# x loaded from the scalar engine's queue, its statistics taken from a copy spread over the partitions, and a shorter PE program: a one-token attention and MLP block on one core

## The chip, the cores and the metric

The kernel runs on one core of one Trainium2 chip. The metric is the device time of one execution in microseconds (us); the core is the only one, so its span is what counts. Lower is better. The engines are named as in the profile: PE (matrix products), PEld (PE's weight loads), DVE (vector), ACT (scalar), POOL (GpSimd) and SP (sync, which here issues transfers). Transfers between HBM and the core's memory run on 16 DMA engines.

## The reference

One token x of 512 numbers is normalised, goes through attention with 32 query heads over a cache of 8 key/value heads of 65536 positions, and beside it through a small MLP; the three are summed.

```python
xn = _layernorm(x)                               # (x - mean) / sqrt(var + 1e-5)
q = (xn @ wq).reshape(B, Sq, Hq, Dh)             # 512 -> 32 heads x 128
scores = einsum("bhqd,bhkd->bhqk", q, k) * Dh ** -0.5
o = einsum("bhqk,bhkd->bhqd", softmax(scores), v)
attention = o.reshape(B, Sq, Hq * Dh) @ wo       # 4096 -> 512
mlp = relu(xn @ w1) @ w2                         # 512 -> 1792 -> 512
return x + attention + mlp
```

All of it is f32. k and v together are 537 million bytes; wq, wo, w1 and w2 are the rest of the 561 MB that the kernel reads.

## The kernel before

The 8 x 65536 cache positions are cut into 32 chunks of 16384 (`NCH`). Two buffers of 128 partitions x 64 KB, `kt` and `vt`, hold one chunk of k and one of v; `kt` first holds wq and last wo, and a third buffer, `wt`, first holds w1 and last w2. There are no copies of these buffers: a buffer is loaded again as soon as its last reader is done, and one is filled while the other is read.

Every engine has its own program, and the order between engines is written out by hand with semaphores. `take(e, sem, n)` makes engine e wait until a semaphore has reached n and takes n off; `after(ins, sem, n)` makes an instruction wait for n; `link` chains POOL's instructions one after another, `next_of` ACT's.

- SP issues all transfers, in this order: the first part of wq (line 151, ahead of the section in which the engines run), xT and xrow (lines 162 and 163: x as 128 partitions x 4 numbers, and x as one row), the other two parts of wq (line 160), w1 (line 164), then k and v in turns (lines 166 to 175), each behind its `kfree` or `vfree`, then wo, w2 and the store of y (line 183).
- POOL fills constants first (lines 195 to 210: `minus` and `plus`, 128 x 128 matrices of -1/512 and 1/512; `eps`; the identity), ends the layer norm (lines 211 to 218: one Newton step on the reciprocal root, xn, and xn into `qpad`), and scales the four quarters of w1 by xn and adds them (lines 223 to 228).
- ACT begins the layer norm on xT (lines 238 to 248): it sums each partition's four numbers, PE multiplies the sums by `minus` (line 267), which gives every partition the negative mean; ACT centres x, squares and sums again, PE multiplies by `plus` (line 268), and ACT adds eps and takes the root. Then ACT copies xrow into `x4`, loads the table for Exp, and in its loop computes the exponentials of each chunk.
- PE runs a loop of 34 turns, `turns`. Turn t multiplies what lies in `kt` by `qpad` (line 314: wq in turn 0, k in turns 1 to 32, wo in turn 33), 8 rounds of 4 products into two pairs of PSUM banks. In turns 2 to 33 there stands ahead of that the second half of the chunk before: the maximum over the partitions (lines 277 and 278), three passes of the MLP's product that give the same result each turn (line 282), the product with `vt` (line 293) and the sums (lines 300 and 303). A hint at the head of the loop is tied to a branch near the end of the program that is always taken.
- DVE clears PSUM (`banks`, line 373), takes the reciprocal root (line 374), transposes PE's scores out of PSUM (line 367), computes the maxima and keeps the running sums. In turn 0 the transposes wait for the third part of wq before they give the banks back (`turn_scores(["wq2", "wq2"])`).

Of the kernel before, what the change touches and what calls it, by code (L numbers as in the profile page):

```python
# [8 lines left out]
AF = mybir.ActivationFunctionType  # L9
# [3 lines left out]
P = 128  # L13
D = 512
# [21 lines left out]
NCH = SK // CHUNK  # L36
NB = CHUNK // P
XA = D // P
WIDE = 4
ROUNDS = 8  # L40
WQ_CUTS = [4096, 4096, 8192]
WQ_SEMS = ["ends", "k", "wq2"]
# [7 lines left out]
def take(e, sem, n=1):  # L50

    return e.sem_inc(sem, -n).wait_op(sem, n, "sem-ge")  # L52
# [7 lines left out]
def attention_and_mlp_kernel(  # L60
# [11 lines left out]
    nc = tc.nc  # L72
    sp, pe, dve, act, pool = nc.sync, nc.tensor, nc.vector, nc.scalar, nc.gpsimd
    scale = float(DH) ** -0.5

    def sbuf(name, *shape):
        return nc.alloc_sbuf_tensor(name, list(shape), F32).ap()
# [3 lines left out]
    def sem(name):  # L81
        if name not in sems:
            sems[name] = nc.alloc_semaphore(name)
        return sems[name]

    def after(ins, name, n=1):

        return ins.wait_op(sem(name), n, "sem-ge")

    kt = sbuf("kt", P, CHUNK)  # L90
# [7 lines left out]
    xrow = sbuf("xrow", 1, D)  # L98
    x4 = sbuf("x4", P, D)
    ident = sbuf("ident", P, P)  # L100
    ones = sbuf("ones", P, P)
    minus = sbuf("minus", P, P)
    plus = sbuf("plus", P, P)
    eps = sbuf("eps", P, 1)
    sel = sbuf("sel", P, WIDE, GROUP)
    xT = sbuf("xT", P, XA)
    st = sbuf("st", P, 8)
    xc = sbuf("xc", P, XA)
    sq = sbuf("sq", P, XA)
    xn = sbuf("xn", P, XA)  # L110
    qpad = sbuf("qpad", P, 32)
    qall = sbuf("qall", P, NQ)
# [15 lines left out]
    banks = nc.alloc_psum_tensor("banks", [P, 8 * 512], F32).ap()  # L128
    pair = [banks[:, i * 1024 : (i + 1) * 1024] for i in range(2)]
    acc = banks[:, 2048:2560]  # L130
    pma = banks[:, 2560:3072]
    lo_new = pma[:, 256 : 256 + 2 * GROUP].rearrange("p (t g) -> p t g", g=GROUP)
    pmb = banks[:, 3072:3584]
    y4 = banks[:, 3584:]
    hrow = y4[:, : FB * 32]
    yacc = acc[:, :P]

    wq_row = wq[0].rearrange("p a n -> p (a n)")
    wo_row = wo[0].rearrange("d j n -> d (j n)")
# [14 lines left out]
    tc.declare_fence(pool.nop().ins, group="first")  # L154
    section = ctx.enter_context(ExitStack())
    inside = section.enter_context(tc.tile_critical(sync_engine=mybir.EngineType.Pool, no_gpsimd_drain=True))  # L156
    for i in range(len(WQ_CUTS)):
        cut = slice(wq_at[i], wq_at[i + 1])
        if i:
            sp.dma_start(kt[:, cut], wq_row[:, cut]).then_inc(sem(WQ_SEMS[i]), 16)  # L160
        else:
            sp.dma_start(xT, x.rearrange("(p a) -> p a", p=P)).then_inc(sem("x"), 16)  # L162
            sp.dma_start(xrow, x.rearrange("(o n) -> o n", o=1)).then_inc(sem("xrow"), 16)  # L163
    sp.dma_start(wt, w1_row).then_inc(sem("w1"), 16)
    take(sp, sem("kfree"))
    sp.dma_start(kt, k[0, 0]).then_inc(sem("k"), 16)
# [8 lines left out]
    for i in range(len(WO_CUTS)):  # L175
        cut = slice(wo_at[i] * D, wo_at[i + 1] * D)
        sp.dma_start(kt[:, cut], wo_row[:, cut]).then_inc(sem(f"wo{i}" if i else "k"), 16)
    sp.wait_ge(sem("hT"), 1)
    for i in range(len(W2_CUTS)):
        cut = slice(w2_at[i] * D, w2_at[i + 1] * D)  # L180
# [7 lines left out]
    def link(ins):  # L188

        if chain[0]:  # L190
            after(ins, "pool", chain[0])
        chain[0] += 1
        return ins.then_inc(sem("pool"), 1)

    pool.memset(minus, -1.0 / D)
    pool.memset(plus, 1.0 / D)
    pool.memset(eps, EPS).then_inc(sem("means"), 1)
    link(pool.memset(ident, 0.0))
    link(pool.affine_select(
# [8 lines left out]
    pool.memset(nb_run, 3.0e38).then_inc(sem("free"), 2)  # L208
    pool.memset(lo_run, 0.0)
    pool.memset(x4, 0.0).then_inc(sem("x4"), 1)  # L210
    pool.wait_ge(sem("ln"), 4)
    link(pool.tensor_mul(st[:, 6:7], st[:, 5:6], st[:, 5:6]))
    link(pool.tensor_mul(st[:, 6:7], st[:, 6:7], st[:, 3:4]))
    link(pool.tensor_scalar(st[:, 6:7], st[:, 6:7], -0.5, 1.5, op0=ALU.mult, op1=ALU.add))
# [18 lines left out]
    def next_of(ins):  # L233

        ins.then_inc(sem("act"), 1)
        take(act, sem("act"))

    act.wait_ge(sem("means"), 1)
    act.wait_ge(sem("zero"), 1)
    act.wait_ge(sem("x"), 16)  # L240
    act.activation(xc, xT, AF.Copy, accum_out=st[:, 0:1]).then_inc(sem("ln"), 1)
    take(act, sem("mean"))
    next_of(act.activation(st[:, 1:2], pma[:, 0:1], AF.Copy))
    next_of(act.activation(xc, xT, AF.Identity, bias=st[:, 1:2]))
    act.activation(sq, xc, AF.Square, accum_out=st[:, 2:3]).then_inc(sem("ln"), 1)
    take(act, sem("mean"))
    next_of(act.activation(st[:, 3:4], pmb[:, 0:1], AF.Identity, bias=eps))
    act.activation(st[:, 4:5], st[:, 3:4], AF.Sqrt).then_inc(sem("ln"), 1)
    act.wait_ge(sem("xrow"), 16)
    act.wait_ge(sem("x4"), 1)  # L250
    act.activation(x4[0:1, :], xrow, AF.Copy)
    act.preload_act_table(AF.Exp)
    with act.Fori(0, NCH):
        take(act, sem("bias"))
        act.activation(corr, diff.unsqueeze(1).to_broadcast([P, 2, GROUP]), AF.Exp).then_inc(sem("kfree"), 1)  # L255
        for g in range(GROUP):
            last = act.activation(  # L257
                probs[:, :, g], tr[:, :, g], AF.Exp, bias=nb_new[:, g : g + 1], scale=scale,
                accum_out=part_sum[:, g : g + 1],
# [4 lines left out]
    kb = kt.rearrange("p (b c e) -> p b c e", c=CT, e=32)  # L264
    hb = wt[:, :f].rearrange("p (b e) -> p b e", e=P)

    after(pe.matmul(pma[:, 0:1], minus, st[:, 0:1], start=True, stop=True), "ln").then_inc(sem("mean"), 1)
    after(pe.matmul(pmb[:, 0:1], plus, st[:, 2:3], start=True, stop=True), "ln", 2).then_inc(sem("mean"), 1)
    turn = nc.alloc_registers("turn", engines=[pe.engine])
    nc.regs_mov(turn, 0)  # L270
    nc.br("turns", engines=[pe.engine])
    with nc.body("turns", valid_engines=[pe.engine]):
        t = nc.snap(turn, min_val=0, max_val=NCH + 1)

        ahead = pe.mark_branch_hint_location()
        with pe.If(t > 1):
            after(pe.transpose(pma[:GROUP, :P], m, ident), "d2p").then_inc(sem("p2d"), 1)  # L277
            after(pe.matmul(pmb[:, :GROUP], ones[:GROUP, :], dg, start=True, stop=True), "d2p", 2).then_inc(sem("p2d"), 1)  # L278

            with pe.Fori(0, PASSES):  # L280
                for c in range(CT):
                    ins = pe.matmul(  # L282
                        hrow[32 * c : 32 * c + 1, :], ones[:, :1], hb[:, :, 32 * c : 32 * c + 32],
                        start=True, stop=True,
                    )
                    if c == 0:
                        after(ins, "sum")
            take(pe, sem("v"), 17)
            n = NB // WIDE
            for i in range(n):  # L290
                c = 32 * (i % CT)
                b = i * WIDE
                last = pe.matmul(  # L293
                    acc[c : c + WIDE * GROUP, :],
                    probs[:, b : b + WIDE, :].rearrange("p b g -> p (b g)"),
                    vt[:, b * DH : (b + WIDE) * DH],
                    start=(i < CT), stop=(i >= n - CT),
                )
            last.then_inc(sem("p2d"), 1)
            pe.matmul(lo_new[:, 0, :], ones, part_sum, start=True, stop=True).then_inc(sem("vfree"), 1)  # L300
            take(pe, sem("d2p"), 3)
            for b in range(WIDE):
                last = pe.matmul(  # L303
                    lo_new[:, 1, :], o_sb[:, b, :], sel[:, b, :],
                    start=(b == 0), stop=(b == WIDE - 1),
                )
            last.then_inc(sem("p2d"), 1)
        take(pe, sem("q"))
        take(pe, sem("k"), 16)
        for s in range(ROUNDS):  # L310
            if s == ROUNDS - 2:
                take(pe, sem("free"), ROUNDS // 2)
            for c in range(CT):
                last = pe.matmul(  # L314
                    pair[s // 2 % 2][32 * c : 32 * c + 32, s % 2 * 512 : s % 2 * 512 + 512], qpad,
                    kb[:, s * 16 : s * 16 + 16, c, :], start=True, stop=True,
                )
                if c == 0 and s % 2 == 0 and s < ROUNDS - 2:
                    after(last, "free", s // 2 + 1)
            if s % 2:  # L320
                last.then_inc(sem("p2d"), 1)
        nc.regs_alu(turn, turn, 1, op=ALU.add)
        pe.br_lt(turn, NCH + 2, on_true="turns", on_false="last")
# [14 lines left out]
    for b in range(W2_ROWS, FB):  # L338
        for c in range(CT):
            last = pe.matmul(  # L340
                yacc[32 * c : 32 * c + 1, :], hT[:, b : b + 1], wt[:, b * D + c * P : b * D + (c + 1) * P],
                start=(b == W2_ROWS), stop=(b == FB - 1),
# [3 lines left out]
        if b + 1 == W2_SUM:  # L346
# [5 lines left out]
            for c in range(CT):  # L352
                ins = pe.matmul(
                    yacc[32 * c : 32 * c + 1, :], ones[:, :1], ysum[:, c * P : (c + 1) * P],
                    start=False, stop=False,
# [6 lines left out]
    def turn_scores(gates=(), free=None):  # L362

        for s in range(ROUNDS // 2):
            if free and s == ROUNDS // 2 - 1:
                after(dve.nop(), "p2d", s + 1).then_inc(sem(free), 1)
            ins = after(dve.transpose(tr2[:, s * 1024 : (s + 1) * 1024], pair[s % 2]), "p2d", s + 1)  # L367
            if s < len(gates):
                ins = after(dve.drain(), gates[s], 16)
            ins.then_inc(sem("free"), 1)  # L370

    dve.memset(ones, 1.0)
    dve.memset(banks, 0.0).then_inc(sem("zero"), 1)
    after(dve.reciprocal(st[:, 5:6], st[:, 4:5]), "ln", 3).then_inc(sem("ln"), 1)
    turn_scores(["wq2", "wq2"], free="kfree")
    dve.drain()
    dve.tensor_reduce(qall, of_own_row(NQ, XA), axis=AX.X, op=ALU.add).then_inc(sem("dve"), 1)
# [77 lines left out]
```

## Time and profile before

| | |
|---|---|
| median of 3 runs | 1303.4 us (1303.09 to 1303.95) |
| the profiled execution, device time | 1303.58 us |
| its span, first to last instruction | 1302.0 us |
| PE busy | 769.7 us, 59% |
| DVE busy | 274.9 us, 21% |
| bytes read from HBM | 560.99 MB |

The profile is of one execution. "Busy" is an engine's own time in instructions. "Releaser" (`<-`) is what the profile takes to have ended a wait; PEq, DVEq and so on are an engine's sequencer. A line number can be that of a helper: L52 is `take`, L367 is `turn_scores`. The span leaves out what lies ahead of the first and behind the last instruction: 1303.58 - 1302.0 = 1.58 us in this execution.

### The profile page before, as it was taken

The numbers are of one execution on the slowest core, as the hardware profiler recorded it, in microseconds if no ns is written. First come the engines' busy times: TensorE is split into PE (matmuls) and PEld (weight loads), VectorE is DVE, ScalarE is ACT, GpSimd is POOL, SyncE is SP. The second block draws the span as 40 slices with busy tenths as digits, with TensorE's granted clock in tenths as the row PEclk, the third lists the DMA queues.
The fourth block names the chain that finished last, engine by engine and source line by source line (L and its number), as shares of the span: only waits on it lengthen the run. The fifth ranks groups of instructions, "written<-read, shape, count | busy, mean of one in ns | idle before, by whom it ended". The sixth has DMA issues, their size and how long they took to land.

```text
span 1302.0 us, 13053 instructions
## 1 busy us (share of the span) xinstructions
PE 769.7 (59%) x5474; PEld 231.0 (18%) x5474; DVE 274.9 (21%) x466; ACT 77.4 (6%) x300; POOL 34.8 (3%) x30
## 2 busy tenths in 40 slices
PE   3365665555665655575566566466566556656667
PEld 1111111111111111121111121111111111112112
DVE  2211222211222221222221122221122221122222
ACT  1000000000000000000000000000000000000000
POOL 1900000000000000000000000000000000000000
PEclk9667876777777777877777787777787776678678
DMA  9999999999999999999999999999999999999998
GB/s 403 449 421 445 425 441 429 431 439 419 451 419 449 421 449 421 441 429 431 439 425 445 419 449 421 449 421 441 429 431 439 425 445 419 451 419 449 421 430 360
DMA packets 11235, 561.02 MB, mean 431 GB/s; under 512 B 1505, under 2 KB 1505, under 8 KB 1890
## 3 DMA queue, kind: packets, MB, share of 16 engines
q1 hardware_dynamic: 11234, 561.00, 99.7%
q8 instruction: 1, 0.02, 0.0%
HBM read 560.99 MB, written 0.00 MB: 431 GB/s over the span
## 4 chain that ended last, share of the span: by engine, by line
issue 94%; DMA 3%; POOL 2%; SPq 0%; PE 0%; DVE 0%; POOLq 0%
DMA wt<-w 3%; POOL wt L223 1%; POOL wt L226 0%; POOL wt L227 0%; POOL wt L228 0%; SPq L181 0%; SPq L160 0%; PE banks L340 0%; DVE ysb L416 0%; SPq L151 0%; SPq L162 0%; SPq L163 0%; POOL hT L230 0%; SPq L451 0%; POOLq L156 0%
## 5 line engine op out<-in xcount | busy, mean ns | idle before, releaser
L314 PE MATMUL banks<-kt,qpad 128*32 128x512 f32 x2176 | 309.4, 732 | 310.5 <-PEq L52 309.2
L293 PE MATMUL banks<-vt,probs 128*16 128x512 f32 x2048 | 269.4, 686 | 87.9 <-PEq L52 87.9
L367 DVE STREAM_TRANSPOSE tr<-banks 128x1024 f32<-128x1024 f32 x136 | 170.0, 1250 | 468.9 <-PE banks L314 466.0
L314 PEld LDWEIGHTS banks<-kt,qpad 128*32 128x32 f32 x2176 | 84.0, 131 | 508.8 <-issue 497.1
L293 PEld LDWEIGHTS banks<-vt,probs 128*16 128x16 f32 x2048 | 69.3, 107 | 301.4 <-issue 301.4
L282 PE MATMUL banks<-wt,ones 128*1 128x448 f32 x768 | 119.2, 774 | 0.0
L393 DVE COPY o_sb<-banks 128x512 f32<-128x512 f32 x32 | 22.1, 692 | 457.0 <-PE banks L293 457.0
L255 ACT ACTIVATE corr<-diff 128x8 f32<-128x8 f32 x32 | 6.7, 209 | 1179.6 <-ACTq L52 1179.6
L257 ACT ACTIVATE probs<-tr,nb_new 128x128 f32<-128x128 f32 x128 | 65.3, 520 | 0.0
L277 PE MATMUL banks<-ident,m 128*4 128x128 f32 x32 | 9.8, 307 | 79.0 <-DVE m L385 79.0
L303 PE MATMUL banks<-sel,o_sb 128*128 128x4 f32 x256 | 32.8, 252 | 18.7 <-PEq L52 18.7
L303 PEld LDWEIGHTS banks<-sel,o_sb 128*128 128x128 f32 x256 | 31.0, 191 | 20.5 <-issue 20.5
L230 POOL TENSOR_SCALAR hT<-ysum 128x14 f32<-128x14 f32 x1 | 0.3, 256 | 1218.4 <-DVE ysum L405 1218.4
L385 DVE TENSOR_REDUCE m<-tr 128x4 f32<-128x512 f32 x32 | 32.2, 1006 | 2.9
L282 PEld LDWEIGHTS banks<-wt,ones 128*1 128x1 f32 x768 | 20.1, 99 | 56.8 <-issue 56.2
L278 PE MATMUL banks<-dg,ones 4*128 4x4 f32 x64 | 14.8, 300 | 20.0 <-DVE dg L388 20.0
L257 ACT ACTIVATION_READ_ACCUMULATOR probs<-tr,nb_new 128x1 f32 x128 | 24.1, 188 | 0.0
L277 PEld LDWEIGHTS banks<-ident,m 128*4 128x4 f32 x32 | 2.6, 81 | 108.0 <-DVE m L385 108.0
L223 POOL TENSOR_SCALAR wt<-wt,xn 128x1792 f32<-128x1792 f32 x4 | 19.1, 4797 | 15.3 <-DMA wt<-w 15.3
L278 PEld LDWEIGHTS banks<-dg,ones 4*128 4x128 f32 x64 | 12.0, 233 | 27.2 <-DVE dg L388 27.2
L300 PEld LDWEIGHTS banks<-part_sum,ones 128*128 128x128 f32 x64 | 9.5, 188 | 27.2 <-issue 27.2
L396 DVE TENSOR_TENSOR lo_run<-lo_run,banks 128x8 f32<-128x8 f32 x32 | 5.2, 163 | 40.0 <-DVEq L52 40.0
(70 smaller groups left out, 92.5 us busy)
## 6 DMA issues: line engine op xcount, KB each, us to landing
kt<-wq SPq DMA_DIRECT2D x2, 2048.0 KB, 9.4
kt<-wq SPq DMA_DIRECT2D x1, 4096.0 KB, 20.8
kt<-wo SPq DMA_DIRECT2D x1, 4096.0 KB, 14.4
kt<-wo SPq DMA_DIRECT2D x2, 2048.0 KB, 21.2
wt<-w SPq DMA_DIRECT2D x1, 3584.0 KB, 28.8
wt<-w SPq DMA_DIRECT2D x1, 1536.0 KB, 11.7
wt<-w SPq DMA_DIRECT2D x1, 1024.0 KB, 13.8
kt<-k SPq DMA_DIRECT2D x32, 24.6
```

The source lines that it names most:

```text
L223: last = pool.tensor_scalar_mul(w1_of[a], w1_of[a], xn[:, a : a + 1])
L257: last = act.activation(probs[:, :, g], tr[:, :, g], AF.Exp, bias=nb_new[:, g : g + 1], scale=scale, accum_out=part_sum[:, g : g + 1],)
L277: after(pe.transpose(pma[:GROUP, :P], m, ident), "d2p").then_inc(sem("p2d"), 1)
L278: after(pe.matmul(pmb[:, :GROUP], ones[:GROUP, :], dg, start=True, stop=True), "d2p", 2).then_inc(sem("p2d"), 1)
L282: ins = pe.matmul(hrow[32 * c : 32 * c + 1, :], ones[:, :1], hb[:, :, 32 * c : 32 * c + 32], start=True, stop=True,)
L293: last = pe.matmul(acc[c : c + WIDE * GROUP, :], probs[:, b : b + WIDE, :].rearrange("p b g -> p (b g)"), vt[:, b * DH : (b + WIDE) * DH], ...
L300: pe.matmul(lo_new[:, 0, :], ones, part_sum, start=True, stop=True).then_inc(sem("vfree"), 1)
L303: last = pe.matmul(lo_new[:, 1, :], o_sb[:, b, :], sel[:, b, :], start=(b == 0), stop=(b == WIDE - 1),)
L314: last = pe.matmul(pair[s // 2 % 2][32 * c : 32 * c + 32, s % 2 * 512 : s % 2 * 512 + 512], qpad, kb[:, s * 16 : s * 16 + 16, c, :], start ...
L367: ins = after(dve.transpose(tr2[:, s * 1024 : (s + 1) * 1024], pair[s % 2]), "p2d", s + 1)
L385: dve.reduce_max(m, tr.rearrange("p b i -> p i b")[:, :GROUP, :], axis=AX.X).then_inc(sem("d2p"), 1)
L393: after(dve.tensor_copy(o_sb.rearrange("p b d -> p (b d)"), acc), "p2d", 7).then_inc(sem("d2p"), 1)
```

## The change

x is loaded by two transfers on ACT's queue, xrow first, at the head of ACT's program; SP's queue no longer has them. PE multiplies a row of 128 ones with xrow, which puts all 512 numbers of x on every partition (`xall`, a PSUM bank). ACT sums them over the columns, with the sum, and after centring the sum of squares, as results on every partition, so the two products with `minus` and `plus` are gone, and the two matrices with them. The table for the root is loaded ahead of the first wait. DVE's clearing of PSUM counts on `xrow`'s semaphore, so the product waits for 16 + 1. In PE's loop the copy of the turn counter into a second register is gone, and a plain compare-and-branch takes the place of the `If`. By the change's own description PE's program then has 449 instructions.

```diff
-    minus = sbuf("minus", P, P)
-    plus = sbuf("plus", P, P)
...
-    sq = sbuf("sq", P, XA)
+    sq = sbuf("sq", P, D)
...
+    xall = pmb
...
-    for i in range(len(WQ_CUTS)):
+    for i in range(1, len(WQ_CUTS)):
         cut = slice(wq_at[i], wq_at[i + 1])
-        if i:
-            sp.dma_start(kt[:, cut], wq_row[:, cut]).then_inc(sem(WQ_SEMS[i]), 16)
-        else:
-            sp.dma_start(xT, x.rearrange("(p a) -> p a", p=P)).then_inc(sem("x"), 16)
-            sp.dma_start(xrow, x.rearrange("(o n) -> o n", o=1)).then_inc(sem("xrow"), 16)
+        sp.dma_start(kt[:, cut], wq_row[:, cut]).then_inc(sem(WQ_SEMS[i]), 16)
...
-    pool.memset(minus, -1.0 / D)
-    pool.memset(plus, 1.0 / D)
     pool.memset(eps, EPS).then_inc(sem("means"), 1)
...
-    pool.wait_ge(sem("ln"), 4)
+    pool.wait_ge(sem("ln"), 3)
...
+    act.dma_start(xrow, x.rearrange("(o n) -> o n", o=1)).then_inc(sem("xrow"), 16)
+    act.dma_start(xT, x.rearrange("(p a) -> p a", p=P)).then_inc(sem("x"), 16)
+    act.preload_act_table(AF.Sqrt)
     act.wait_ge(sem("means"), 1)
-    act.wait_ge(sem("zero"), 1)
+    take(act, sem("xall"))
+    next_of(act.activation(sq, xall, AF.Copy, accum_out=st[:, 0:1]))
+    next_of(act.activation(st[:, 1:2], st[:, 0:1], AF.Copy, scale=-1.0 / D))
+    next_of(act.activation(sq, xall, AF.Square, bias=st[:, 1:2], accum_out=st[:, 2:3]))
+    next_of(act.activation(st[:, 3:4], st[:, 2:3], AF.Identity, bias=eps, scale=1.0 / D))
+    act.activation(st[:, 4:5], st[:, 3:4], AF.Sqrt).then_inc(sem("ln"), 1)
     act.wait_ge(sem("x"), 16)
-    act.activation(xc, xT, AF.Copy, accum_out=st[:, 0:1]).then_inc(sem("ln"), 1)
-    take(act, sem("mean"))
-    next_of(act.activation(st[:, 1:2], pma[:, 0:1], AF.Copy))
-    next_of(act.activation(xc, xT, AF.Identity, bias=st[:, 1:2]))
-    act.activation(sq, xc, AF.Square, accum_out=st[:, 2:3]).then_inc(sem("ln"), 1)
-    take(act, sem("mean"))
-    next_of(act.activation(st[:, 3:4], pmb[:, 0:1], AF.Identity, bias=eps))
-    act.activation(st[:, 4:5], st[:, 3:4], AF.Sqrt).then_inc(sem("ln"), 1)
-    act.wait_ge(sem("xrow"), 16)
+    act.activation(xc, xT, AF.Identity, bias=st[:, 1:2]).then_inc(sem("ln"), 1)
     act.wait_ge(sem("x4"), 1)
...
-    after(pe.matmul(pma[:, 0:1], minus, st[:, 0:1], start=True, stop=True), "ln").then_inc(sem("mean"), 1)
-    after(pe.matmul(pmb[:, 0:1], plus, st[:, 2:3], start=True, stop=True), "ln", 2).then_inc(sem("mean"), 1)
+    after(pe.matmul(xall, ones[0:1, :], xrow, start=True, stop=True), "xrow", 17).then_inc(sem("xall"), 1)
...
-        t = nc.snap(turn, min_val=0, max_val=NCH + 1)
...
-        with pe.If(t > 1):
+        pe.br_lt(turn, 2, on_true="scores", on_false="values")
+        with nc.body("values", valid_engines=[pe.engine]):
...
             last.then_inc(sem("p2d"), 1)
+            nc.br("scores", engines=[pe.engine])
+        nc.switch_bb("scores")
...
-    dve.memset(banks, 0.0).then_inc(sem("zero"), 1)
-    after(dve.reciprocal(st[:, 5:6], st[:, 4:5]), "ln", 3).then_inc(sem("ln"), 1)
+    dve.memset(banks, 0.0).then_inc(sem("xrow"), 1)
+    after(dve.reciprocal(st[:, 5:6], st[:, 4:5]), "ln").then_inc(sem("ln"), 1)
```

## The prediction

> **What bounds the kernel now.** I read the page first, for which engine never rests, and then stretches of the span, to see whether that holds everywhere.
>
> ```profile
> span 1302.0 us, 13053 instructions
> ...
> PE 769.7 (59%) x5474; PEld 231.0 (18%) x5474; DVE 274.9 (21%) x466; ACT 77.4 (6%) x300; POOL 34.8 (3%) x30
> ...
> DMA  9999999999999999999999999999999999999998
> ...
> q1 hardware_dynamic: 11234, 561.00, 99.7%
> q8 instruction: 1, 0.02, 0.0%
> ```
>
> No compute engine is busy more than 59% of the span, while one DMA queue, SP's, keeps all 16 DMA engines at 99.7%. The stretches (columns: busy time of PE, PEld, DVE, ACT, POOL, then PE's clock, DMA share, GB/s) show where the remaining 0.3% lies:
>
> ```profile
> 0.00:2.00 2.00, 0.00 (x0) 0.00 (x0) 0.17 (x1) 0.00 (x0) 1.00 (x9) 1.00 0.44 98
> 2.00:6.00 4.00, 0.00 (x0) 0.00 (x0) 3.47 (x1) 0.00 (x0) 1.25 (x7) 1.00 0.86 348
> 6.00:8.00 2.00, 0.00 (x0) 0.00 (x0) 0.00 (x0) 0.00 (x0) 0.00 (x0) 1.00 1.03 420
> 8.00:14.00 6.00, 1.17 (x4) 1.00 (x4) 0.00 (x0) 3.56 (x9) 0.00 (x0) 1.00 1.09 464
> 14.00:28.00 14.00, 8.91 (x64) 2.30 (x64) 4.69 (x5) 2.33 (x4) 1.26 (x6) 1.00 0.98 422
> 28.00:32.00 4.00, 0.00 (x0) 0.00 (x0) 1.01 (x3) 0.00 (x0) 0.09 (x1) 0.80 1.17 499
> 32.00:64.00 32.00, 9.39 (x71) 3.07 (x75) 6.73 (x9) 0.00 (x0) 30.96 (x7) 0.65 0.98 426
> 64.00:1266.00 1202.00, 723.57 (x5127) 217.05 (x5123) 249.60 (x433) 70.09 (x283) 0.00 (x0) 0.75 1.00 434
> ```
>
> From 64 to 1266 us the share is 1.00 at 434 GB/s: nothing to gain there. Ahead of 64 us the shares times their lengths add up to 0.88 + 3.44 + 2.06 + 6.54 + 13.72 + 4.68 + 31.36 = 62.7 us of 64: 1.3 us are missing, and the first two rows alone lack 1.7 us, so the hole is the start-up of the first transfer and not a gap behind it (shares above 1 count overlapping packets).
>
> **The change, part by part.** First the two loads of x, which leave SP's queue for ACT's:
>
> ```profile
> 0.73 0.39 SPq L151 DMA_DIRECT2D kt<-wq  x1
> 1.35 0.33 SPq L162 DMA_DIRECT2D xT<-x  x1
> 1.74 0.33 SPq L163 DMA_DIRECT2D xrow<-x  x1
> 2.12 0.90 SPq L160 DMA_DIRECT2D kt<-wq  x2
> 3.05 0.48 SPq L164 DMA_DIRECT2D wt<-w  x1
> 8.56 1.28 ACT L241 ACT_TABLE_LOAD   x1 [8.56 <-DMA xT<-x]
> ```
>
> SP issues the second and third parts of wq, and w1, 2.12 - 1.35 = 0.77 us sooner. That is sequencer time only: the first part (L151, untouched) is 2048 KB (2.1 MB), which at 434 GB/s occupies the engines for 4.8 us; 98 GB/s over the first 2 us is 0.2 MB, so data flow from about 1.5 to 6.3 us, while the second part is on the queue by 2.5 us already. So the 0.77 us lie under that transfer and are worth 0; without it they would be worth 0.77. The 2 KB twice over of x still pass the same engines, on a second queue. Price: at worst a 0.6 us hiccup (a 16 KB row at 434/16 GB/s), at best 1.3 us, the whole missing share of the start. I take a gain of 0.1, close to nothing, because most of that hole stands ahead of the first packet.
>
> Then the layer norm. Before, x waits behind the first wq part, and the statistics make two trips over PE:
>
> ```profile
> 2.11 3.47 DVE L373 MEMSET banks<- 128x4096 f32 x1 [0.85 <-issue]
> 10.20 0.59 PE L267 MATMUL banks<-st,minus 128*128 128x1 f32 x2 [10.20 <-ACT xc L241]
> 14.34 0.20 ACT L248 ACTIVATE st<-st 128x1 f32<-128x1 f32 x1
> 14.45 0.61 ACT L251 ACTIVATE x<-xrow 1x512 f32<-1x512 f32 x1
> 16.38 0.19 POOL L218 COPY qpad<-xn 128x4 f32<-128x4 f32 x1
> 16.86 5.27 PE L314 MATMUL banks<-kt,qpad 128*32 128x512 f32 x32 [4.30 <-PEq L52]
> 23.44 1.25 DVE L367 STREAM_TRANSPOSE tr<-banks 128x1024 f32<-128x1024 f32 x1 [1.71 <-DMA kt<-wq]
> 27.23 0.33 SPq L166 DMA_DIRECT2D kt<-k  x1
> 31.91 19.12 POOL L223 TENSOR_SCALAR wt<-wt,xn 128x1792 f32<-128x1792 f32 x4 [15.35 <-DMA wt<-w]
> ```
>
> After: ACT issues at about 1.1 to 1.9 us. A small transfer on quiet engines lands in 1.4 us; xT, behind 2 MB, took 7.1:
>
> ```profile
> xT<-x SPq DMA_DIRECT2D x1, 2.0 KB, 7.1
> y<-ysb SPq DMA_DIRECT2D x1, 2.0 KB, 1.4
> ```
>
> So xrow lands between 2.5 and 8.6 us; I take the early end, since a queue of its own has nothing large ahead in it. The product also waits for the clearing of PSUM, which ends at 5.58. Two passes of a 512-column product:
>
> ```profile
> L314 PE MATMUL banks<-kt,qpad 128*32 128x512 f32 x2176 | 309.4, 732 | 310.5 <-PEq L52 309.2 <-DVEq L369 1.3
> L257 ACT ACTIVATE probs<-tr,nb_new 128x128 f32<-128x128 f32 x128 | 65.3, 520 | 0.0
> L257 ACT ACTIVATION_READ_ACCUMULATOR probs<-tr,nb_new 128x1 f32 x128 | 24.1, 188 | 0.0
> ```
>
> 2 x 0.73 = 1.5 us, so x stands in PSUM at 7.1. No row has ACT over 128x512; 128x128 with a bias takes 0.52, 1x512 0.61, so 0.6 plus 0.19 for the accumulator, twice, and as the high bound four times the 0.52. With the three one-column steps (0.2 to 0.26 each) and 0.1 us between steps that is 2.8 us: root done at 9.9, and from the root's end to qpad's end it was 16.57 - 14.54 = 2.0: q is ready at 11.9 instead of 16.57. With both high bounds (xrow at 8.6, 2.1 us per pass over x) it is 8.6 + 1.5 + 5.8 + 2.0 = 17.9. The table of the root is now loaded while ACT waits for PE; one table load fewer (1.28 us) lies in the chain.
>
> What is late next? PE takes the second wq part, on the engines until about 1.5 + 4.2 MB / 434 GB/s = 11.2, then DVE waits 1.71 us for the third part: the row at 23.44 says so. q's 4.7 us therefore vanish in that wait. And k's issue at 27.23 itself is ahead of need: w1 lands at 31.8, so k stands 4.6 us in the queue. Gain 0. The cover: q may be 1.7 us later than it was, 18.3, before wq's third part is no longer what ends last, and 4.6 - 1.4 = 3.2 later still, 21.5, before the engines run dry; beyond that each us of q costs one.
>
> POOL loses two memsets (0.2 each) ahead of its chain, and waits for three steps of the norm instead of four; DVE's reciprocal waits for ACT's root as before. Behind ACT's new wait for PE stand only the norm, the copy of xrow and the load of the Exp table, needed first at 64 us. PE's new wait holds back turn 0, which waits for q anyway. All at 0 under w1's transfer.
>
> In the loop PE loses one register move a turn. The slack there:
>
> ```profile
> 1227.44 0.33 SPq L171 DMA_DIRECT2D kt<-k  x1
> 1231.70 8.84 PE L293 MATMUL banks<-vt,probs 128*16 128x512 f32 x64 [0.83 <-PEq L52]
> 1240.95 0.34 SPq L173 DMA_DIRECT2D vt<-v  x1
> 1251.05 9.41 PE L314 MATMUL banks<-kt,qpad 128*32 128x512 f32 x64 [8.58 <-PEq L52]
> ```
>
> k is queued 4.3 us before the v ahead of it is in use, v 10.1 us before. So nothing under 3 us a turn (4.3 less the 1.4 of a quiet transfer's latency) reaches the end: 0.
>
> The end. PE's program gets 5 instructions shorter: one f32 product fewer (two weight loads, two matmuls, as L267's x2 shows) and the register move.
>
> ```profile
> q8 instruction: 1, 0.02, 5.8%
> ...
> 1299.46 0.34 SPq L183 DMA_DIRECT2D y<-ysb  x1
> ...
> SPq L451 <- PEq L451: 1.4, 2, 1.1
> ```
>
> The first row is the stretch 1298 to 1299 us: the only instruction packet of the execution, 16 KB, 5.8% of 16 engines for 1 us = 0.93 us of one engine. After it SP waits up to 1.1 us for PE's sequencer in the closing barrier. My reading, not shown by a row: the last few instructions of PE stand in the piece that is fetched there, and five fewer may keep them ahead of it. y lands at 1299.46 + 1.4 = 1300.9, and the barrier can't close before that, so most of the 1.1 us is covered. Gain from 0 to 1.1; I take 0.15.
>
> [...]
>
> **Sum.** 1302.0 - 0.1 - 0.15 = 1301.75 us of span; the execution took 1303.58, 1.58 more, so 1303.3, and the median of the runs is 0.18 below that execution: 1303.2.
>
> **The rivals.**
> (1) Nothing changes at all: the late piece of PE's program stays, x's place is worth nothing. 1303.4. For it: the 99.7%. It can hardly be told from the forecast.
> [...]
> (3) x, on its own queue, is served only when SP's queue is empty, behind w1 at 31.8. Then q comes at 31.8 + 1.5 + 2.8 + 2.0 = 38.1, the wq product follows in 27.23 - 16.86 - 1.7 = 8.7, k is issued at 47 and the engines stand idle from 31.8 to 48: +16, 1319. It decides when x lands later than about 21.5 - 6.3 = 15. No row has two busy queues.
> [...]
> (4) The fetch at the end is put off until PE runs out of instructions behind the last product. Then it is exposed: from its packet's stretch (about 1298.5) to y's landing at 1300.9 it was covered, 2.4 us, with a 1.4 us latency ahead of it 3.8: 1305.8 to 1307.2. [...]
>
> **How the numbers follow.** Forecast 0.62, (1) 0.27, (2) 0.04, (3) 0.03, (4) 0.04. About 0.2% (2.6 us) is what a measurement of this kernel can tell from no change. A gain of that size would need more than both upper bounds together (1.3 + 1.1 = 2.4): 0.01, taken out of the forecast's share. Within: 0.61 + 0.27 = 0.88. Slower: 0.11. The range covers the forecast and (1): low, half of the two upper bounds, 1303.4 - 1.2 = 1302.2; high, the slowest run shown (1303.95) plus the hiccup of 0.6: 1304.6. It leaves out (2) to (4).
>
> **What would show it.** In the changed kernel's profile: xT and xrow landing before 5.6 us, PE's first product at about 5.6, qpad written near 12; DVE's second transpose still waiting for wq near 23.4; k issued near 27 and w1 in use near 31.9; 1.00 of DMA share from 64 on. An instruction packet in each turn, x after 31 us, or SP's closing wait grown by 2 us would prove me wrong.

## The result, and the profile after

| | before | changed |
|---|---|---|
| median, 22 runs each | 1303.38 us | 1305.13 us |
| lowest to highest | 1302.93 to 1304.39 | 1303.00 to 1310.36 |
| ratio, 95% interval | | 1.0015 (1.0008 to 1.0021) |
| the profiled execution | 1303.58, span 1302.0 | 1304.83, span 1303.1 |

The change made the kernel 0.15% slower. Its best run is within 0.1 us of the best one before; what grew is the spread. It looks as if something now happens late in many executions, and by a different amount in each.

The page of the changed kernel still shows a stream that hardly rests; q10 is ACT's queue:

```profile
span 1303.1 us, 13010 instructions
...
q1 hardware_dynamic: 11088, 561.00, 99.6%
q10 hardware_dynamic: 146, 0.00, 0.0%
```

The start of the changed kernel, in order of time (start, length, engine and line, and in brackets how long the engine had been idle and what ended it):

```profile
1.34 0.81 SPq L158 DMA_DIRECT2D kt<-wq  x2
...
1.54 0.37 ACTq L232 DMA_DIRECT2D xT<-x  x1
...
5.64 2.07 PE L260 MATMUL banks<-xrow,ones 1*128 1x512 f32 x2 [5.64 <-DVE banks L367]
...
12.50 0.19 POOL L211 COPY qpad<-xn 128x4 f32<-128x4 f32 x1
13.13 6.03 PE L308 MATMUL banks<-kt,qpad 128*32 128x512 f32 x32 [5.42 <-PEq L52]
...
22.79 6.31 PE L308 MATMUL banks<-kt,qpad 128*32 128x512 f32 x32 [3.64 <-DVEq L363]
...
29.30 0.33 SPq L161 DMA_DIRECT2D kt<-k  x1
...
31.29 19.13 POOL L216 TENSOR_SCALAR wt<-wt,xn 128x1792 f32<-128x1792 f32 x4 [18.60 <-DMA wt<-w]
52.21 8.85 PE L308 MATMUL banks<-kt,qpad 128*32 128x512 f32 x64 [23.11 <-PEq L52]
```

Two rows of the kernel before, from the same stretch:

```profile
51.51 8.44 PE L314 MATMUL banks<-kt,qpad 128*32 128x512 f32 x64 [24.47 <-PEq L52]
...
64.87 0.34 SPq L171 DMA_DIRECT2D kt<-k  x1
```

Read the two kernels side by side. q is ready at 12.69 instead of 16.57, not far from the 11.9 of the forecast, and PE begins wq 3.7 us sooner. It then has to wait for wq's third part in either kernel; that wait now lasts 3.64 us instead of 1.27. The same 32 products behind it take 6.31 us; they took 3.64. k, which is queued when they end, is queued at 29.30 instead of 27.23. w1 is in use 0.6 us sooner than before, and yet k's first chunk comes into use 0.70 us later, at 52.21 instead of 51.51: from w1 to k it is 20.9 us instead of 19.6. The next k is then queued at 65.96 instead of 64.87, 1.1 us later, and that is the whole difference between the two spans. The profiled execution lost its time here. The stretches of the two kernels (columns: busy time of PE, PEld, DVE, ACT, POOL, then PE's granted clock, DMA share, GB/s), before first:

```profile
20.00:23.00 3.00, 2.13 (x20) 0.41 (x12) 1.25 (x1) 0.00 (x0) 0.00 (x0) 1.00 0.85 367
23.00:28.00 5.00, 3.64 (x32) 0.96 (x32) 3.28 (x3) 0.00 (x0) 0.00 (x0) 1.00 1.01 436
```

```profile
20.00:23.00 3.00, 0.21 (x4) 0.20 (x8) 0.17 (x1) 0.00 (x0) 0.00 (x0) 0.73 0.87 375
23.00:28.00 5.00, 5.00 (x28) 1.07 (x24) 2.33 (x2) 0.00 (x0) 0.00 (x0) 0.50 1.00 430
```

The granted clock was 0.50 from 23 to 28 us in the changed kernel, where the second half of the wq product runs, and 1.00 there before.

### The profile page after: what moved, and what is told of

It is laid out like the page before. It is cut to its first block, busy times and chain, and to the rows that moved or that the text cites. A ratio compares the mean times of both kernels' runs of the same rounds, so it can differ in the third digit from the quotient of the medians.

```text
span 1303.1 us, 13010 instructions
## 1 busy us (share of the span) xinstructions
PE 775.1 (59%) x5472; PEld 231.9 (18%) x5472; DVE 274.8 (21%) x466; ACT 77.9 (6%) x299; POOL 34.5 (3%) x28
## 3 DMA queue, kind: packets, MB, share of 16 engines
q1 hardware_dynamic: 11088, 561.00, 99.6%
## 4 chain that ended last, share of the span: by engine, by line
issue 94%; DMA 3%; POOL 2%; SPq 0%; PE 0%; DVE 0%; POOLq 0%
DMA wt<-w 3%; POOL wt L216 1%; POOL wt L221 0%; POOL wt L220 0%; POOL wt L219 0%; PE banks L334 0%; SPq L176 0%; SPq L158 0%; DVE ysb L410 0%; PE banks L347 0%; SPq L150 0%; POOL hT L223 0%; SPq L445 0%; POOLq L155 0%
## 5 line engine op out<-in xcount | busy, mean ns | idle before, releaser
L308 PE MATMUL banks<-kt,qpad 128*32 128x512 f32 x2176 | 313.0, 739 | 308.7 <-PEq L52 305.0
L285 PE MATMUL banks<-vt,probs 128*16 128x512 f32 x2048 | 273.4, 695 | 91.3 <-PEq L52 91.3
L274 PE MATMUL banks<-wt,ones 128*1 128x448 f32 x768 | 116.5, 759 | 0.0
```

Source lines behind the costliest of these rows:

```text
L274: ins = pe.matmul(hrow[32 * c : 32 * c + 1, :], ones[:, :1], hb[:, :, 32 * c : 32 * c + 32], start=True, stop=True,)
L285: last = pe.matmul(acc[c : c + WIDE * GROUP, :], probs[:, b : b + WIDE, :].rearrange("p b g -> p (b g)"), vt[:, b * DH : (b + WIDE) * DH], ...
L308: last = pe.matmul(pair[s // 2 % 2][32 * c : 32 * c + 32, s % 2 * 512 : s % 2 * 512 + 512], qpad, kb[:, s * 16 : s * 16 + 16, c, :], start ...
```

## The experiments

Twelve runs follow, of the changed kernel once more and of eleven edited ones, each timed beside the kernel before on the same chip. The theory to be tested, T1: PE, served earlier, idles longer ahead of wq's third part; its clock falls in that gap; the second half runs slowly; k is queued too late to follow w1 without a gap. Its rivals: the second queue disturbs the stream (T2), PE's new program costs something in each turn (T3), the late k only accompanies a loss with another cause (T4).

**The changed kernel again, and three partial ones.** Nothing is edited in the first.

> The changed kernel once more, as control and for a second profile. Three theories. T1 (clock): the earlier layer norm moves PE's half of the wq product into 13 to 19 us; PE's granted clock then drops to 0.5 while the second half runs, k's issue slips from 27.2 to 29 us or later and comes too late for the end of w1, so the DMA engines run dry once, near 30 us. T2 (second queue): the transfers of x on ACT's queue interleave with wq's and disturb the stream. T3 (PE's program): the rearranged loop costs a little each turn. T1: 1305 median, spread of several us, the second half of the wq product again near 6 us, k's issue at 29 or later. T2: the same time, but with the loss before 25 us. T3: the loss spread over 64 to 1266 us.

1304.65 us (1302.94 to 1309.47, ratio 1.0016, 1.0007 to 1.0025). Its profiled execution is one of the longer ones, span 1305.6:

```profile
13.64 6.35 PE L308 MATMUL banks<-kt,qpad 128*32 128x512 f32 x32 [5.93 <-PEq L52]
...
22.76 5.21 PE L308 MATMUL banks<-kt,qpad 128*32 128x512 f32 x32 [2.77 <-DVEq L363]
...
28.17 0.33 SPq L161 DMA_DIRECT2D kt<-k  x1
...
52.92 9.08 PE L308 MATMUL banks<-kt,qpad 128*32 128x512 f32 x64 [24.95 <-PEq L52]
...
66.89 0.34 SPq L166 DMA_DIRECT2D kt<-k  x1
```

Here the gap was 2.77 us and only part of the second half, until 25.97 us, ran at half clock; k was queued 1.1 us sooner than in the first profile, and its first chunk was nevertheless 0.7 us later in use. So the expected k's issue "at 29 or later" was not met, and the size of the loss does not follow the lateness alone. A part of the loss came later: the stretch from 64 to 300 us moved 431 GB/s, and 435 in the kernel before (the rows stand below).

Next, the changed kernel with q held back:

```diff
+    for _ in range(7):
+        link(pool.memset(ysum, 0.0))
     take(pool, sem("ends"), 16)
     after(pool.tensor_copy(qpad[:, :XA], xn), "pool", chain[0]).then_inc(sem("q"), 1)
```

> The changed kernel with q held back: seven fills of 128x512 on POOL ahead of the copy into qpad, about 4.3 us, so that PE begins the wq product near 17 us as before the change. Nothing else differs. T1: the clock is full again during the second half, k is issued near 26.7 us, and since wq and w1 land 0.6 us sooner than before the change, 1302.8 with a narrow spread. T2 and T3: 1305 as in the changed kernel.

1303.42 us (1303.14 to 1304.68, ratio 1.0003, 0.9994 to 1.0012): the spread is gone, with the second queue, the spread product and the new branch all in place.

```profile
17.31 4.99 PE L310 MATMUL banks<-kt,qpad 128*32 128x512 f32 x32 [9.60 <-PEq L52]
22.59 3.64 PE L310 MATMUL banks<-kt,qpad 128*32 128x512 f32 x32 [0.29 <-DVEq L365]
26.43 0.33 SPq L161 DMA_DIRECT2D kt<-k  x1
...
50.50 8.90 PE L310 MATMUL banks<-kt,qpad 128*32 128x512 f32 x64 [24.26 <-PEq L52]
```

PE starts 4.2 us later than in the changed kernel and is done 2.9 us sooner. T2 and T3 fall as the cause. The gain that was expected on top, 1302.8, did not come: the median span is 1301.4 and that of the kernel before 1301.6, but what lies outside the span is 2.0 us instead of 1.6; why was not pursued.

The kernel before with x on ACT's queue alone:

```diff
-        else:
-            sp.dma_start(xT, x.rearrange("(p a) -> p a", p=P)).then_inc(sem("x"), 16)
-            sp.dma_start(xrow, x.rearrange("(o n) -> o n", o=1)).then_inc(sem("xrow"), 16)
...
+    act.dma_start(xrow, x.rearrange("(o n) -> o n", o=1)).then_inc(sem("xrow"), 16)
+    act.dma_start(xT, x.rearrange("(p a) -> p a", p=P)).then_inc(sem("x"), 16)
     act.wait_ge(sem("means"), 1)
```

> The kernel before with the two loads of x on ACT's queue and nothing else. xT lands near 10.1 us there (in the changed kernel's profile the small packets take turns with wq's) instead of 8.5, so q comes near 18 us. T1: no loss, wq and w1 land 0.6 us sooner, 1302.8 to 1303.4, narrow spread. T2: 1305.

1306.33 us (1303.29 to 1311.01, ratio 1.0022, 1.0012 to 1.0032), with a median above that of the whole change, though the intervals overlap. The expectation missed, but the profile shows how k comes to be late:

```profile
12.60 0.58 PE L266 MATMUL banks<-st,minus 128*128 128x1 f32 x2 [12.60 <-ACT xc L240]
...
18.78 0.19 POOL L215 COPY qpad<-xn 128x4 f32<-128x4 f32 x1
19.26 9.98 PE L313 MATMUL banks<-kt,qpad 128*32 128x512 f32 x64 [4.31 <-PEq L52]
...
24.35 0.23 PEld L313 LDWEIGHTS banks<-kt,qpad 128*32 128x32 f32 x4 [0.63 <-issue]
25.19 0.14 PEld L313 LDWEIGHTS banks<-kt,qpad 128*32 128x32 f32 x4 [0.61 <-issue]
25.62 0.14 PEld L313 LDWEIGHTS banks<-kt,qpad 128*32 128x32 f32 x4 [0.29 <-issue]
...
29.43 0.33 SPq L163 DMA_DIRECT2D kt<-k  x1
```

q comes at 18.97, not far from the 18 of the expectation, and that is already too late: the wq product then runs without a gap, ends at 29.2, and k is queued at 29.43. The expectation had taken over the prediction's 3.2 us of cover. The product itself is slower too, 9.98 us for 64 products where before it was 5.27 + 3.64 = 8.91. Its weight loads tell why: they come every 0.85 us until 25.2 us and every 0.43 us from then on; before, the change is at 20.2 us. So PE, idle for 4.31 us until then, begins the wq product at half its later pace, and does so in every kernel here, behind 4.30 to 10.28 us of idle time. The view of the granted clock doesn't show it: the traces' first record of the clock stands at 25.2 us here and at 20.2 before, and ahead of that the view says 1.00. So k can be late because PE slows down in the middle of the product, or because x is late and PE starts late; both give the same wide spread (1303.00 to 1310.36 us and 1303.29 to 1311.01).

The branch alone, in the kernel before:

```diff
-        t = nc.snap(turn, min_val=0, max_val=NCH + 1)
 
         ahead = pe.mark_branch_hint_location()
-        with pe.If(t > 1):
+        pe.br_lt(turn, 2, on_true="scores", on_false="values")
+        with nc.body("values", valid_engines=[pe.engine]):
...
+            nc.br("scores", engines=[pe.engine])
+        nc.switch_bb("scores")
```

> The kernel before with the plain branch in PE's loop and without the copied counter, nothing else. T1 and T2: 1303.3, as before. T3: 1305.

1303.20 us (1302.91 to 1304.46, ratio 1.0000, 0.9991 to 1.0009). PE's loop costs and gains nothing.

**k's lateness by itself, and the gap by itself.** The kernel before with only the release of kt put off:

```diff
-                after(dve.nop(), "p2d", s + 1).then_inc(sem(free), 1)
+                after(dve.memset(ysum, 0.0), "p2d", s + 1)
+                dve.memset(o_sb, 0.0)
+                dve.memset(yd, 0.0)
+                dve.memset(probs, 0.0).then_inc(sem(free), 1)
```

> The kernel before with nothing changed but the moment at which kt is given free in turn 0: four fills of 128x512 on DVE (about 0.45 us each) stand ahead of it, so k's first issue moves from about 27.0 to 28.8 us. T1 with a slack of 1 us: 1304 to 1306 and a spread of several us, as in the changed kernel. With the slack of 3.2 us that the prediction gave: 1303.3, no change.

1304.69 us (1304.01 to 1308.38, ratio 1.0018, 1.0009 to 1.0027): loss and spread of the changed kernel, from 1.4 us of delay in one release, without its queue, product or branch.

```profile
22.59 3.64 PE L314 MATMUL banks<-kt,qpad 128*32 128x512 f32 x32 [0.51 <-DVEq L372]
...
28.65 0.33 SPq L166 DMA_DIRECT2D kt<-k  x1
...
51.68 8.53 PE L314 MATMUL banks<-kt,qpad 128*32 128x512 f32 x64 [25.45 <-PEq L52]
```

T4 falls. Now the changed kernel with three products in the gap:

```diff
+            if s == ROUNDS // 2:
+                pe.br_lt(turn, 1, on_true="warm", on_false="rest")
+                with nc.body("warm", valid_engines=[pe.engine]):
+                    for _ in range(3):
+                        pe.matmul(acc[:32, :], qpad, kt[:, :512], start=True, stop=True)
+                    nc.br("rest", engines=[pe.engine])
+                nc.switch_bb("rest")
```

> The changed kernel with three more products of 512 columns in turn 0, between the two halves of the wq product (they write a PSUM bank that nobody reads in that turn), so that PE is idle there for about 1 us instead of 3.6. T1 in the form that the idle gap lets the granted clock fall: the clock stays 1.0 until about 30 us, the second half takes about 3.7 us, k is issued near 26.7, 1303.0 to 1303.4 with a narrow spread. If it is PE's early start and not the gap, the clock still drops near 21 us and the time stays at 1304.7 or above.

1305.59 us (1305.38 to 1306.04, ratio 1.0019, 1.0010 to 1.0028). The start is as T1 says: PE as early as in the changed kernel, but idle for 0.95 us only, and the second half back at 3.64:

```profile
13.27 6.18 PE L315 MATMUL banks<-kt,qpad 128*32 128x512 f32 x32 [5.56 <-PEq L52]
...
19.27 2.74 PE L309 MATMUL banks<-kt,qpad 128*32 128x512 f32 x6
22.96 3.64 PE L315 MATMUL banks<-kt,qpad 128*32 128x512 f32 x32 [0.95 <-DVEq L370]
26.79 0.33 SPq L161 DMA_DIRECT2D kt<-k  x1
```

So in this kernel it is the gap and not the early start that costs the clock. The time is nevertheless high, but with a spread of 0.66 us: a fixed price at another place, at the very end:

```profile
1298.09 0.60 PE L341 MATMUL banks<-wt,hT 128*1 128x128 f32 x12
1300.70 0.39 PE L341 MATMUL banks<-wt,hT 128*1 128x128 f32 x4 [2.01 <-issue]
```

PE stands for 2.0 us ahead of its last four products with nothing to wait for. This kernel's PE program has 462 instructions. A later kernel tests that.

x back on SP's queue, with all else of the change kept:

> The changed kernel with the two loads of x back on SP's queue at their old place; the spread product, ACT's sums and the branch stay. x lands near 8.5 us, so q comes near 15.5 instead of 12.5 and PE's first half ends near 21: an idle gap of about 2 us ahead of the second half. T1: the clock stays full, k is issued near 27, 1303.2 with a narrow spread. If the spread product itself is what costs: 1304.7.

1303.41 us (1303.07 to 1303.96, ratio 1.0001, 0.9992 to 1.0010).

```profile
15.42 5.17 PE L308 MATMUL banks<-kt,qpad 128*32 128x512 f32 x32 [5.20 <-PEq L52]
22.91 3.64 PE L308 MATMUL banks<-kt,qpad 128*32 128x512 f32 x32 [2.32 <-DVEq L363]
26.74 0.33 SPq L163 DMA_DIRECT2D kt<-k  x1
```

A gap of 2.32 us left the clock alone; 2.77 us, in the second profile of the changed kernel, cost it for part of the half. The length of the gap does not decide by itself, though. The loop of the kernel before has a gap of 2.47 us in each turn. Two of them, and the 3 us behind each (the granted clock is the last number but two):

```profile
140.28 0.27 PE L277 MATMUL banks<-ident,m 128*4 128x128 f32 x1 [2.47 <-DVE m L385]
...
140.28:143.28 3.00, 2.38 (x23) 0.89 (x27) 0.99 (x5) 1.01 (x4) 0.00 (x0) 1.00 0.81 350
```

```profile
102.14 0.37 PE L277 MATMUL banks<-ident,m 128*4 128x128 f32 x1 [2.47 <-DVE m L385]
...
102.14:105.14 3.00, 2.38 (x15) 0.87 (x19) 0.99 (x5) 0.69 (x4) 0.00 (x0) 0.50 0.81 350
```

Of 32 such gaps, all begun at full clock, 10 kept it until 3 us behind their end; in or behind the other 22 it fell. In the traces of the kernel before and of the changed kernel it changes in steps: the stretches at one clock are 3.41 to 23.89 us long, and each but the last, which ends with the trace, is a multiple of 3.41 us. In the wq product it was half from 21.39 to 28.22 us in the first profile of the changed kernel and from 22.56 to 25.97 in the second, 6.83 and 3.41 us. So where a gap lies against these steps matters beside its length: the 10 gaps that kept the clock began 1.57 to 1.80 us behind an edge of this 3.41 us grid, the other 22 between 0.64 and 1.25 or between 2.15 and 2.33 us behind one. And a gap's loss differs from one execution to the next: 6.31 us for the second half in the first profile, 5.21 in the second.

**Ways around it.** The changed kernel with k's first chunk in two halves:

```diff
-    take(sp, sem("kfree"))
-    sp.dma_start(kt, k[0, 0]).then_inc(sem("k"), 16)
+    half = CHUNK // 2
+    sp.wait_ge(sem("p2d"), 2)
+    sp.dma_start(kt[:, :half], k[0, 0][:, :half]).then_inc(sem("khalf"), 16)
+    take(sp, sem("kfree"))
+    sp.dma_start(kt[:, half:], k[0, 0][:, half:]).then_inc(sem("k"), 16)
...
+    dve.wait_ge(sem("khalf"), 16)
     take(dve, sem("p2d"), 4)
```

> The changed kernel with the first k chunk loaded in two halves: SP issues the first half (columns 0 to 8191 of kt) as soon as PE has finished its first four rounds of the wq product, near 19 to 20 us, and the second half where the whole was issued before. Theory T1 says that the change loses only because k's first issue comes too late for the end of w1; here 4 MB (9.7 us) lie ahead of the late half, so PE may still run its second half at half clock and it costs nothing: 1302.9 or a little less, spread under 1.5 us, all 16 engines within 0.5 us of each other at the end of k's first chunk. Rival T4: the loss comes of the second queue or of the clock in later turns, and k's first issue only accompanies it: 1304.6 to 1305 as in the changed kernel.

```profile
22.69 5.34 PE L311 MATMUL banks<-kt,qpad 128*32 128x512 f32 x32 [4.13 <-DVEq L366]
28.22 0.33 SPq L164 DMA_DIRECT2D kt<-k  x1
...
50.67 9.07 PE L311 MATMUL banks<-kt,qpad 128*32 128x512 f32 x64 [22.64 <-PEq L52]
...
y<-ysb SPq DMA_DIRECT2D x1, 2.0 KB, 2.6
```

The half clock is still there (5.34 us) and costs nothing at this place: k comes into use at 50.67, 1.5 us sooner than in the changed kernel, and the spread is 1.0 us (1304.10 to 1305.14). The median of 1304.54 (ratio 1.0009, 1.0000 to 1.0018) is not what was expected, since the store of y took 2.6 us to land, against 1.4 before. A further kernel took one transfer off SP's queue again:

```diff
-WO_CUTS = [16, 8, 8]
+WO_CUTS = [16, 16]
...
-    turn_scores(["wo1", "wo2"])
+    turn_scores(["wo1", "wo1"])
```

> The kernel with k's first chunk in two halves, and wo loaded in two parts instead of three, so that SP issues as many transfers in all as the changed kernel does. In split_k the stream ran through without a dent, yet the store of y took 2.6 us to land instead of 1.4. If the number of transfers on SP's queue is what does that, the store lands in 1.4 us again: 1303.0, spread under 1 us, a shade under the kernel before. If not, 1304.5 as in split_k.

1303.89 us (1303.50 to 1305.54, ratio 1.0005, 0.9996 to 1.0014). The store lands in 1.4 us again, as was expected if the number of transfers decides. But it can't be the number alone: the kernel before has 79 transfers on SP's queue, the kernel with k in two halves 78 and this one 77, and before the store landed in 1.4 us as well. And the new cut opens another gap, at the end, with the effect known by now. The profiled execution, 1305.47 us, is one of the three long ones of eleven (1305.26 to 1305.54; the others 1303.50 to 1303.95):

```profile
1289.55 5.34 PE L311 MATMUL banks<-kt,qpad 128*32 128x512 f32 x32 [2.38 <-DVEq L366]
...
1301.48 0.34 SPq L181 DMA_DIRECT2D y<-ysb  x1
```

The second half of the wo product ran as one burst of 5.34 us behind a gap of 2.38 us, and the store went out 2.3 us later than in the kernel with wo in three parts (1299.20). What the clock did in the eight shorter executions no trace shows.

Last, wq cut elsewhere (`WQ_CUTS = [4096, 8192, 4096]`), in the changed kernel, in the kernel before, and in the changed kernel with three products more behind PE's loop:

> The changed kernel with wq's three parts cut at 4096 + 8192 + 4096 columns instead of 4096 + 4096 + 8192, nothing else. PE's first half waits for the second part, which now lands near 17 us instead of 13, so q may be early and PE still starts late: first half from about 17 to 22, then the third part near 22.4, no idle gap. T1: clock 1.0 through the second half (3.6 us), k issued near 26.4, all engines within 0.5 us at the end of k's first chunk, 1302.7 to 1303.2 with a narrow spread. Rival: any loss that comes of the second queue, of the spread product or of PE's program stays: 1304.7.

> The kernel before with the same cut. There q comes at 16.6 us already, so nothing should move: 1303.2. Beside recut it tells what x on ACT's queue is worth when PE's clock is kept: by the spread of the engines at the end of w1 (0.3 to 0.5 us with x aside, 0.5 to 1.1 with x in line) up to 0.5 us.

> The recut kernel with three small products added behind PE's loop, into a bank that nobody reads any more and while PE waits for w2: PE's program has 461 instructions instead of 449. In the run with products in the gap (462 instructions) PE stood idle for 2.0 us ahead of its last four products, with nothing to wait for. If that is the late piece of the program, it shows again here: the store of y 2 to 2.5 us later, 1305.2, narrow spread. If it was something of that run, 1303.0.

Recut: 1303.57 us (1303.08 to 1304.76, ratio 1.0003, 0.9994 to 1.0012); the kernel before, recut: 1303.39 us (1302.88 to 1304.52, 1.0001, 0.9992 to 1.0010). The cut takes the loss away, by a constant, and x's place is then worth nothing that shows. Neither recut nor hold_q beats the kernel before. The product of recut is one burst without a gap:

```profile
17.99 9.56 PE L308 MATMUL banks<-kt,qpad 128*32 128x512 f32 x64 [10.28 <-PEq L52]
```

It took 9.56 us, since PE again began at half pace (loads every 0.85 us until 23.1), so k was queued at 27.74 and not near 26.4 as expected. With the three products, 461 instructions: 1306.07 us (1305.28 to 1306.76, ratio 1.0020, 1.0011 to 1.0029), and an idle time of nearly the same length at the same place:

```profile
1300.83 0.53 PE L336 MATMUL banks<-wt,hT 128*1 128x128 f32 x3 [2.19 <-issue]
```

**The runs side by side.** Each of the 16 engines closes its share of a transfer with a 4-byte packet (16 of them from 30.30 to 31.40 us, at the end of w1 before), and the trace has the time of each. From these, the first and the last engine to end w1 and k's first chunk, in us (one profiled execution of each kernel; the median is that of all its runs):

```
kernel         k queued   w1 ends          lead   k's chunk ends   behind by   median
hold_q           26.43    30.25 to 30.56   3.82   49.59 to 49.90     0.31      1303.42
spread_only      26.74    30.27 to 30.93   3.53   49.60 to 50.25     0.65      1303.41
branch_only      26.81    30.38 to 30.85   3.57   49.71 to 50.17     0.46      1303.20
before           27.23    30.30 to 31.40   3.07   49.76 to 50.72     0.96      1303.38
recut            27.74    30.22 to 30.88   2.48   49.55 to 50.19     0.64      1303.57
changed, 2nd     28.17    30.31 to 30.72   2.14   49.78 to 52.45     2.67      1304.65
late_k           28.65    30.27 to 30.57   1.62   49.86 to 50.97     1.11      1304.69
changed, 1st     29.30    30.27 to 30.73   0.97   50.26 to 51.75     1.49      1305.13
queue_only       29.43    30.35 to 30.70   0.92   50.42 to 51.28     0.86      1306.33
```

"Lead" is the time from k's issue to the first engine's end of w1, "behind by" the distance between the first and the last engine behind k's chunk. With a lead of 2.48 us or more the engines come out no further apart than they went in; with 2.14 or less the last one ends later than 50.9, and they come out further apart. It is not the distance that costs, since before they are 0.96 apart throughout, but the end: in the two latest rows even the first engine is late (50.26 and 50.42, elsewhere 49.55 to 49.86), and in the second profile of the changed kernel one engine alone is, the other 15 ending by 50.12. The engines stay apart (the last section has the numbers), and every chunk is ready only when the last has landed: in the second profile the last engine ends k's first chunk at 52.45, and PE takes it up at 52.92. That eats the lead of the following issues. In the second profile of the changed kernel the next k was queued at 66.89, and the first engine was through with v at 69.10, a lead of 2.2 again, where it is 69.09 - 64.87 = 4.2 in the kernel before. The loss then repeats; the two rows are of that profile and of before:

```profile
64.00:300.00 236.00, 143.41 (x1009) 42.51 (x1013) 49.43 (x88) 14.72 (x59) 0.00 (x0) 0.75 1.00 431
```

```profile
64.00:300.00 236.00, 142.56 (x1014) 42.41 (x1006) 48.35 (x84) 15.61 (x63) 0.00 (x0) 0.75 1.01 435
```

4 GB/s less over 236 us are 236 x 4 / 435 = 2.2 us. From 300 us on both move 433 GB/s, with the engines of that profile still 1.8 us apart at 342 us. This is how one late issue can cost between nothing and 7 us. How far a given lateness throws the engines apart differs from one execution to the next, and what decides that is open.

## Why the prediction was wrong, point by point

- **What bounds the kernel: right; the two small gains: not seen in the time.** The stream sets the time (SP's queue fills 99.7% of the 16 engines' span before and 99.6% in the changed kernel). SP's earlier issues and x's place are worth nothing by themselves: recut and the kernel before with the same cut differ by 0.18 us, the wrong way and within their intervals. PE's closing was as read: in the trace's control instructions PE enters the last barrier at 1301.14 before, 2.2 us behind its last product and behind the landing of y, and at 1300.18 in the changed kernel, 0.2 behind its last product and ahead of the store. From y's landing to the end of the span it is then 1.10 us before and 0.97 in both profiles of the changed kernel. But what lies outside the span grew from 1.6 to 1.7 us in the mean of the runs, so no gain in the time is shown.
- **x lands early: half wrong.** xrow, one packet, was there before PSUM was clear (PE's row at 5.64 waits for DVE). xT took 9.0 us from its issue, where it had taken 7.1 behind the first part of wq: each of its 16-byte packets took turns with a 16 KB packet. On each engine one came every 0.61 us, which is the median time of one 16 KB packet there. In the changed kernel this was still in time for the step that needs it at 10.57; in queue_only it made q 2.4 us later than before and cost about as much as the whole change. Rival (3) fell by it: xT was there at 10.5 us in the first profile, and not behind w1's 31. But taking turns is not being early when the transfer has many packets, 128 here.
- **q at 11.9: nearly right** (12.69), and the layer norm's parts with it, except that the two passes of the spread product took 2.07 us and not 1.5.
- **The step that failed is "q's 4.7 us therefore vanish in that wait ... Gain 0".** The wait is not empty: a longer wait of PE is an idle gap, and the clock fell to half inside it, at 21.39 us in the first profile and at 22.56 in the second. The forecast took the second half's 3.64 us as given. It became 6.31 with a gap of 3.64, 5.21 with 2.77, 5.34 with 4.13 (split_k), and stayed 3.64 with 2.32, 1.27, 0.95 and 0.29. The prediction's row of 14 to 28 us has 1.00 for PE's clock, but PE's weight loads in that stretch come at half pace until 20.2 us (every 0.85 us, then every 0.43): that PE slows down was there to be seen. In these runs a gap of 2.32 us kept the clock, gaps of 2.38 (at the end of split_k_wo) and 2.77 lost it for a part of the burst, and 2.47 in the loop did either. Those gaps of 2.47 us are in the trace of the kernel before, and in or behind 22 of the 32 the clock fell: that spoke against this change, and the prediction did not weigh it.
- **The cover was mis-sized, 3.2 us against some 0.7.** It was measured from k's issue to w1's first use (4.6) less the latency of a lone small store (1.4). By the table above the stream needs the next transfer 2.1 to 2.5 us ahead, and ahead of the first engine's end (30.30), not of w1's use (31.91): 3.07 less 2.1 to 2.5 leaves 0.6 to 1.0. The prediction watched for an instruction packet in each turn (the changed kernel's trace has a single one of 16 KB in the whole span), a starved x and a late fetch, and not for a k that comes a little late, because the cover seemed ample.
- **The range** (1302.2 to 1304.6) ended below the median of 1305.13. The loss is within the 0.2% that was called the most likely outcome, but it is a loss clear of noise, not the gain of 0.2 us.
- **Rival (4) did not occur, but a pause of the size it gave did in two edited kernels:** with twelve instructions more than in recut, PE's last products stood behind one of 2.2 us. With 454 and with 449 instructions there is none in front of a product. In the kernel with 462 the one instruction packet of 16 KB near the end begins between 1298.00 and 1298.75 us, and the pause lasts from 1298.69 to 1300.70; that PE waits for it is argued from this, not shown.

## What to carry to other kernels

An engine that is handed its input earlier is not free to wait: if its burst is cut in two by a later arrival, look at how long the gap becomes and at what clock the second part then runs (here 3.64 us instead of 1.27, and 0.50 instead of 1.00 from 23 to 28 us). Count the slack of a queued transfer from its issue to the end of the first DMA engine's share of the transfer ahead, less what the queue needs (here 2.1 to 2.5 us), and not to the landing that a consumer sees. When a change widens the spread of the times and leaves the best time alone, look for a hand-over that has become a race.

## What the runs showed of the hardware

- The granted clock fell to half at idle gaps of PE of 2.77, 3.64 and 4.13 us in the middle of a product, and not at one of 2.32; behind one of 2.38 PE's weight loads came every 0.85 us, and later every 0.43. The 32 products behind these gaps took 5.21 to 6.31 us instead of 3.64. The length alone does not decide: at the same gap of 2.47 us in the loop the clock held in 10 turns of 32. In the kernel before and the changed kernel it changed in steps of 3.41 us.
- Behind 4.30 to 10.28 us of idle time PE began the wq product at half pace (weight loads every 0.85 us, later every 0.43), where the view of the granted clock says 1.00 for want of a record.
- In the first profile of the changed kernel the engines, once thrown apart, stayed apart: 1.49 us behind k's first chunk, and still 1.28 us more than a thousand microseconds later (1269.58 to 1270.86).
- Small packets on a second queue were served one by one between the large ones, one every 0.61 us on each engine: 2 KB in 128 pieces took 9.0 us, and 7.1 on the queue of the large ones, behind 2 MB.
- A PE program of 461 or 462 instructions paused for 2.0 to 2.2 us near its end with nothing in the profile to wait for; one of 449 or 454 did not pause there.
- One transfer more on SP's queue than in the changed kernel went along with a store that landed in 2.6 us, and taking another off brought it back to 1.4; with two more, in the kernel before, it was 1.4 too. The cause is open.
